# Batch 0 of a gated-attention and mixer kernel: four columns at a time, and the next batch's z turned by TensorE

## The chip, the cores and the metric

The kernel runs on one core of one Trainium2 chip. The metric is the device time of one execution in microseconds (us). The engines are TensorE (PE in the profile, its weight loads PEld), VectorE (DVE), ScalarE (ACT), GpSimd (POOL) and SyncE (SP). POOL issues the plain and the casting DMAs here, SP the DMA transposes.

## The reference: what is computed

There are 8 batches of 3136 rows. All inputs and the output are float32.

```python
# u, v: (8, 3136, 256), z: (8, 3136, 64), U: (3136, 32), V: (32, 3136)
scores = (z @ z.transpose(0, 2, 1)) / 3136
x = u * (maximum(scores, 0) ** 2 @ v)          # gated attention, no softmax
h = x.transpose(0, 2, 1) @ U @ V               # low-rank mixing along the rows
y = x + h.transpose(0, 2, 1)
out = y + maximum(y @ w_ch1, 0) @ w_ch2        # w_ch1: (256, 1024), w_ch2: (1024, 256)
```

## The kernel before: tiles, stages and the order of the work

**Tiles.** A batch's rows make 25 tiles: tile t below 24 holds rows 24p + t for the 128 partitions p (each partition reads 24 rows that lie together), tile 24 the last 64 rows, twice, one copy in each half of the partitions. All matmuls are in bf16. z is kept turned and doubled (`zT`): channels on the partitions, 64 in each half, a tile of 128 columns for each of the 25 tiles, and the first 12 tiles again behind them, so that a window of columns can run past the end (`extend_z`).

**Scores.** The score matrix is symmetric. For tile j, `A[j]` holds 13 blocks of 128 columns: the columns of tiles j, j+1, ..., j+12, round the ring of 25. `score` (line 286) makes a piece of such a row: two matmuls, each on one half of the partitions, into a pair of PSUM banks (`pair_psum`, two pairs in turn), then ScalarE takes relu and scale out of PSUM into `A[j]` (L311), and VectorE squares it in place (L313). `score_steps(b, j, k0, k1)` cuts the blocks k0 to k1 of row j into pieces of up to 1024 columns. The other 12 blocks of a column come by symmetry: `turn` (L333) has SP transpose `A[o]` blocks 1 to 12 into a `strip` (a pool of 5).

**Outputs.** Output tiles are taken in the order 12, 13, ..., 24, 0, ..., 11. "Output i" is the i-th in this order, tile (12 + i) mod 25; so output 8 is tile 20, output 12 is tile 24 and output 13 is tile 0. An output is 25 products with v, each split in two halves of 64 rows (L371), 49 matmuls in all: the first 13 read blocks of `A`, the last 12 the strip. Output 12, the short tile, uses 64x64 pieces (L405). Two outputs share a pair of accumulators; `close_pair` adds the two halves (ScalarE L385, VectorE L386), multiplies by u (L395) and writes x. For the short tile it also adds the two halves of the partitions (L391, L392).

**The list of an output.** Everything is in an order written out by hand. `attend_steps` gives the steps of an output, and `_spread` puts "fill" between them: score pieces that later outputs, or the next batch, need (`own_at`, `next_at`, for batch 0 `first_at`). The strip of output i + 4 is asked for at the end of output i; in batch 0 `first_turns` says which. In batches from 1 on, the mixing and the two weight products of the batch before are done in bursts after outputs 4, 8, 13 and 17 (`burst_at`).

**The start of batch 0** (`start_up`, L665) has no scores to begin with. TensorE is kept busy by 7 dummy matmuls, turns the first 16 tiles of z against a unit matrix (`turn_on_pe`, L223, with a copy out of PSUM by ScalarE or VectorE, L231), and then outputs 0 to 3 are made together: for each pair of tiles j the scores of four columns, then their products (`make`, `use`). The last 9 tiles of z are doubled at step 3 (`double_z`, L188) and turned at step 5. Beside it run the full rows of tiles 16 to 19 (`nxt`). Outputs 4 to 7 follow in the same way (`make_stored`, `use_stored`); here the scores are stored in `A`, and beside them run the rows of tiles 20 to 22 (`more`) and all that rows 8 to 15 still lack (`rest`). After that output 8 begins the regular loop.

**SP's queue** in this stretch is in program order: a small DMA (`mark`, L729) that reads the third part of batch 1's v and so waits until it has landed, strips of tiles 16 to 19, the two transposes of batch 1's z (`turn_z`, L195), strips of tiles 20, 21, and so on.

**POOL's queue** loads in batch 0: v, z, u for two pairs, batch 1's z, the weights (`weight_steps`: w_ch1, U, V, then w_ch2 in two DMAs), three parts of batch 1's v; then u for each pair, with the other six parts of batch 1's v at outputs 9, 11, 13, 15, 18 and 21 (`v_at`). In each later batch the next z is loaded at output 1, doubled in the burst after output 4, and turned at outputs 7 and 10.

The lines of the start-up that the change rewrites (FIRST is 12, NG 4, LEAD 16, NB 13):

```python
        rest = []
        for j in reversed(range(FIRST - NG, LEAD)):
            rest += score_steps(0, j, LEAD + NG - j, NB)
        more = [s for j in range(LEAD + NG, LEAD + 2 * NG - 1) for s in score_steps(0, j)]
...
            if B > 1 and i in (1, 2):
                part = ((0, FIRST), (FIRST, NF))[i - 1]
                double_z(1, (part,))
                turn_z(1, (part,))
            if i == len(pairs) - 1:
                turn(0, LEAD + NG)
```

Of the kernel before, what the change touches and what calls it, by code (L numbers as in the profile page):

```python
# [10 lines left out]
ALU = mybir.AluOpType  # L11
# [31 lines left out]
def kernel(  # L43
# [17 lines left out]
    P = 128  # L61
# [156 lines left out]
    def turn_on_pe(parts, banks):  # L218

        z_bf = z_tiles[0]  # L220
        for (t0, t1), ps in zip(parts, banks):
            for t in range(t0, t1):
# [9 lines left out]
                out=zT_first[:, t0:t1, :].rearrange("p t c -> p (t c)"),  # L232
# [19 lines left out]
    def weight_steps():  # L252
        def wide(w_bf, w):
            pool_dma(out=w_bf, in_=w.rearrange("(t p) d -> p t d", p=P))
# [19 lines left out]
        def copies():  # L274
            for n in (R, 2 * R):
                nc.vector.tensor_copy(out=V_bf[n : 2 * n, :], in_=V_bf[:n, :])

        fetches = [
            lambda: wide(w1_bf, moe_w_ch1),
            narrow,  # L280
            fetch,
            lambda: wide(w2_bf[:, NH // 2 :, :], moe_w_ch2[H // 2 :, :]),
            lambda: wide(w2_bf[:, : NH // 2, :], moe_w_ch2[: H // 2, :]),
        ]
        third = FIRST // 2
        puts = [lambda t=t: put(t, t + third) for t in range(0, NF, third)]
        return fetches, puts + [put_tail, copies]
# [92 lines left out]
    def close_pair(b, o):  # L380
# [8 lines left out]
        if o == NF:  # L389
# [274 lines left out]

    def start_up():  # L665
# [60 lines left out]
        for i, pair in enumerate(pairs):  # L726
# [3 lines left out]
            if i == 3:  # L730
                double_z(0, parts[2:])
            if i == 5:
# [27 lines left out]
        def make_stored(pair):  # L760
            todo = []
            for j in pair:
                k0, k1 = LEAD - j, min(NB, LEAD + NG - j)
                todo.append((j, LEAD * P, (k1 - k0) * P, A[j][:, k0 * P : k1 * P]))
            score(0, todo)

        nxt += [lambda pair=pair: make_stored(pair) for pair in pairs[:2]]
# [8 lines left out]
        rest = []  # L776
        for j in reversed(range(FIRST - NG, LEAD)):
            rest += score_steps(0, j, LEAD + NG - j, NB)
        more = [s for j in range(LEAD + NG, LEAD + 2 * NG - 1) for s in score_steps(0, j)]
        for i, pair in enumerate(pairs):  # L780
            if i + 2 < len(pairs):
                make_stored(pairs[i + 2])
            else:
                more.pop(0)()
            use_stored(pair, outs)
            if B > 1 and i in (1, 2):
                part = ((0, FIRST), (FIRST, NF))[i - 1]
                double_z(1, (part,))
                turn_z(1, (part,))
# [30 lines left out]
    first_at = {8: [(NT - 2, 0, NB), (0, 0, NB)], 9: [(NT - 1, 0, NB)], 10: [(1, 0, NB)]}  # L820
    first_at.update({11: [(2, 0, NB)], 12: []})
    for j, i in zip(range(3, FIRST), (10, 11, 11, 12, 12, 12, 12, 12, 12)):
        first_at[i].append((j, 0, FIRST - j))
    first_turns = {8: (NT - 2,), 9: (NT - 1, 0)}

    next_at = {i: [] for i in range(NT)}
# [119 lines left out]
```

## Time and profile before

| | |
|---|---|
| timed runs (4) | median 1001.18 us, 999.04 to 1002.29 |
| the profiled execution | 998.98 us |
| its span, first to last instruction | 997.2 us |
| mean granted TensorE clock | 0.998 |
| VectorE, ScalarE busy | 550.8, 612.2 us |
| score relu, L311 (ScalarE) | 477 in 358.9 us |
| strips, L333 (SP) | 196 transposes, median 5.4 us from issue to landing |
| DMA | 167.94 MB, mean 168 GB/s |

How to read it: the page gives busy time per engine, a chain of waits followed back from the last instruction, and the costliest groups of instructions by line. A group's line is `line engine op out<-in`, count, busy time and mean, then the engine's idle time before it and what ended it. Windows give busy time of each engine in a stretch, with the count of instructions in brackets, then the granted TensorE clock, the DMA share and GB/s. In the timeline, rows show start, length, engine and line, and in square brackets the idle time before and its releaser. The ring of DMA engines is shared by all queues.

### The profile page before, as it was taken

To read this page: it belongs to the slowest core of one execution; us is meant where nothing else is said; L and a number is where in the kernel's file an instruction comes from. 1 tells how busy PE (TensorE), PEld (TensorE's weight loads), DVE (VectorE), ACT (ScalarE), POOL (GpSimd) and SP (SyncE) were. 2 spreads that over 40 slices of the span, in tenths; PEclk is the share of its full clock that TensorE was granted. 3 is DMA by queue.
4 is the path that set the end of the run, shared out by engine and by line. 5 is a ranking of instruction groups with operands and counts; after the bars stand their busy time and mean duration, and the time that the engine had idled before them with its cause. 6 is when DMAs were issued, how large, how long until landed. Compare 5 with 4: busy or idle time off the path is not lost.

```text
span 997.2 us, 31020 instructions
## 1 busy us (share of the span) xinstructions
PE 984.4 (99%) x13688; PEld 776.4 (78%) x13688; DVE 550.8 (55%) x1003; ACT 612.2 (61%) x835; POOL 171.8 (17%) x317
## 2 busy tenths in 40 slices
PE   8899999999999999999999999999999999999998
PEld 6678777787778878788787887878877788787866
DVE  6868754456544664456644566445664457542352
ACT  7877764667645776456764667556674666643154
POOL 5111112121121111221112211112111120011000
PEclk9999999999999999999999999999999999999999
DMA  9999989999797998899999997989979998678533
GB/s 188 188 188 203 176 151 188 191 176 180 139 210 163 176 155 179 181 184 170 163 179 171 183 170 147 195 173 176 176 150 196 178 176 159 122 153 161 126 96 100
DMA packets 414790, 167.94 MB, mean 168 GB/s; under 512 B 389488, under 2 KB 399408, under 8 KB 414656
## 3 DMA queue, kind: packets, MB, share of 16 engines
q1 hardware_dynamic: 385424, 99.68, 61.8%
q0 software_dynamic: 29232, 66.28, 28.4%
q8 instruction: 107, 1.75, 0.7%
q14 instruction: 27, 0.22, 0.1%
HBM read 61.88 MB, written 25.69 MB: 88 GB/s over the span
## 4 chain that ended last, share of the span: by engine, by line
PE 95%; ACT 2%; DMA 2%; DVE 1%; POOL 0%; issue 0%; DVEq 0%; POOLq 0%
PE ps L371 50%; PE ps L563 17%; PE ps L610 17%; PE ps L298 7%; ACT A L311 2%; PE ps L531 1%; PE ps L405 1%; DMA strip<-A 1%; DMA z_c<-in_z_dram 1%; PE ps L479 1%; DVE A L313 0%; PE ps L462 0%; ACT both L385 0%; POOL v L244 0%; DVE relu_bf L231 0%
## 5 line engine op out<-in xcount | busy, mean ns | idle before, releaser
L311 ACT ACTIVATE A<-ps 128x832 bf16<-128x832 f32 (+9 forms) x477 | 358.9, 769 | 154.6 <-PE ps L298 146.2
L371 PE MATMUL ps<-v,A 64*128 64x256 bf16 x4988 | 341.3, 270 | 1.2 <-DVE A L313 1.1
L313 DVE TENSOR_TENSOR A<-A 128x832 bf16<-128x832 bf16 (+9 forms) x477 | 244.8, 526 | 135.5 <-ACT A L311 133.3
L371 PE MATMUL ps<-v,strip 64*128 64x256 bf16 x4420 | 307.6, 270 | 2.5 <-DMA strip<-A 2.4
L371 PEld LDWEIGHTS <-A 64*128 64x128 bf16 x4988 | 246.1, 94 | 45.8 <-issue 9.5
L581 ACT ACTIVATE relu_bf<-ps 128x1024 bf16<-128x1024 f32 (+2 forms) x206 | 186.2, 911 | 140.2 <-PE ps L563 140.1
L371 PEld LDWEIGHTS <-strip 64*128 64x128 bf16 x4420 | 221.9, 94 | 37.1 <-DMA strip<-A 3.3
L624 DVE TENSOR_TENSOR o_sb<-ps,x_bf 128x512 f32<-128x512 f32 (+2 forms) x105 | 69.8, 665 | 240.3 <-PE ps L610 225.4
L610 PE MATMUL ps<-w_bf,relu_bf 128*128 128x256 bf16 (+1 forms) x1600 | 201.2, 273 | 0.0
L563 PE MATMUL ps<-ut,w_bf 128*128 128x512 bf16 (+2 forms) x896 | 198.6, 353 | 0.0
L610 PEld LDWEIGHTS <-relu_bf 128*128 128x128 bf16 (+1 forms) x1600 | 153.0, 98 | 45.6 <-issue 3.6
L563 PEld LDWEIGHTS <-w_bf 128*128 128x128 bf16 x896 | 84.9, 98 | 62.0 <-issue 6.9
L355 POOL DMA_DIRECT2D u_sb<-in_u_dram x96 | 53.7, 559 | 453.4 <-DVE x_bf L395 438.9
L298 PE MATMUL ps<-zT 64*128 64x416 bf16 (+8 forms) x812 | 131.6, 312 | 0.0
L385 ACT COPY both<-ps 128x512 f32<-128x512 f32 (+1 forms) x104 | 58.9, 566 | 72.2 <-PE ps L371 65.9
L637 POOL DMA_DIRECT2D out_dram<-o_sb x84 | 46.0, 548 | 272.6 <-DVE o_sb L624 269.3
L386 DVE TENSOR_TENSOR both<-ps,both 128x512 f32<-128x512 f32 (+1 forms) x104 | 69.3, 666 | 28.2 <-ACT both L385 27.5
L395 DVE TENSOR_TENSOR x_bf<-both,u_sb 128x512 bf16<-128x512 f32 (+1 forms) x104 | 69.8, 671 | 3.6
L545 DVE TENSOR_TENSOR x_bf<-ps,x_bf 128x512 bf16<-128x512 f32 (+1 forms) x112 | 65.4, 625 | 7.4 <-PE ps L531 7.3
L298 PEld LDWEIGHTS <-zT 64*128 64x128 bf16 x812 | 43.0, 94 | 4.0
L244 POOL DMA_DIRECT2D v<-in_v_dram x61 | 34.1, 561 | 0.8 <-DMA w_bf<-in_moe_w_ch_dram 0.7
L298 PE MATMUL ps<-relu_bf 64*128 64x416 bf16 (+9 forms) x121 | 22.0, 336 | 4.1 <-ACT A L311 3.3
(54 smaller groups left out, 207.1 us busy)
## 6 DMA issues: line engine op xcount, KB each, us to landing
u_sb<-in_u_dram POOLq DMA_DIRECT2D x96, 256.0 KB, 4.0
out_dram<-o_sb POOLq DMA_DIRECT2D x84, 256.0 KB, 3.1
v<-in_v_dram POOLq DMA_DIRECT2D x57, 192.0 KB, 4.7
strip<-A SPq DMA_TRANSPOSE x196, 5.4
out_dram<-o_sb SPq DMA_DIRECT2D x11, 256.0 KB, 2.0
z_c<-in_z_dram POOLq DMA_DIRECT2D x7, 384.0 KB, 5.9
u_sb<-in_u_dram POOLq DMA_DIRECT2D x16, 64.0 KB, 2.3
ut<-x_bf SPq DMA_TRANSPOSE x56, 3.8
```

Source lines behind the costliest of these rows:

```text
L298: mm(out=ps[:, k, :n], lhsT=zT[halves[k], j, :], rhs=zT_flat[halves[k], c : c + n], start=True, stop=True,)
L311: nc.scalar.activation(out=dst, in_=src, func=AF.Relu, scale=sc)
L313: nc.vector.tensor_tensor(out=dst, in0=dst, in1=dst, op=ALU.mult)
L371: mm(out=acc[t0][h][:, (o - t0) * D : (o - t0 + 1) * D], lhsT=w[halves[h]], rhs=v_both[b % 2][halves[h], j, :], start=start, stop=stop, **kw,)
L385: nc.scalar.copy(out=both[:, :w], in_=banks[1][:, :w])
L386: nc.vector.tensor_tensor(out=both[:, :w], in0=banks[0][:, :w], in1=both[:, :w], op=ALU.add)
L395: nc.vector.tensor_tensor(out=x_at(b, t0, n), in0=split(both[:, :w]), in1=u_sb[:, :n, :].rearrange("p t (a c) -> p t a c", c=P), op=ALU.mult,)
L545: nc.vector.tensor_tensor(out=q, in0=split(ps[h][:, : len(ks) * D]), in1=q, op=ALU.add)
L563: mm(out=ps[i][:, :w] if apart else ps[:, i, :w], lhsT=w1_bf[:, db, (hp + i) * P : (hp + i + 1) * P], rhs=uT[c][:, db, len(chunks[c]) * P ...
L581: nc.scalar.activation(out=relus[c][:, hp : hp + 2, :w], in_=ps[:, :, :w], func=AF.Relu)
L610: mm(out=ps[r, k * D : (k + 1) * D], lhsT=relus[c][:, ht, q : q + (TAIL if two else P)], rhs=w2_bf[:, ht, :], start=(ht < 1 + two), stop=( ...
L624: nc.vector.tensor_tensor(out=o_sb[:p].rearrange("p t (a c) -> p t a c", c=P), in0=split(ps[:p, k0 * D : (k + 1) * D]), in1=x_at(b, t, nk) ...
```

## The change

It touches batch 0 and the first outputs of batch 1.

- Batch 1's z is no longer turned by SP in the start-up. It is doubled at output 9 (VectorE) and turned by TensorE, eight tiles at outputs 10, 11 and 13 and one at 14 (`on_pe`), with copies out of PSUM by ScalarE (tiles 0 to 15 and 24) and VectorE (16 to 23). Its 12 repeated tiles are written at output 15 and no longer at 11.
- `make_stored` takes the column from which four outputs' scores are made. `rest` holds only the blocks for outputs 8 to 11, for two rows at a time; the blocks of rows 12 to 15 for later outputs are made at outputs 8 and 9 (`first_more`).
- The rows of tiles 0 to 11 are spread over outputs 10 to 14 (`first_at`), one full row in each of outputs 8 to 12, and the strips are asked for one output later (`first_turns`). Batch 1's rows are made at outputs 16 to 24 (`after_first`) and no longer from 13.
- In the start-up the last 9 tiles of z are doubled at step 4 and turned at step 6, each one step later.
- w_ch2 comes in one DMA, with 8 rows that lie together on each partition, and w_ch1 is loaded into a part of `x_bf` and its columns are put in the matching order by VectorE after outputs 19 and 20 (`order_w`).
- In batch 0 the short tile adds the halves of its partitions straight out of PSUM: four VectorE adds in place of two ScalarE copies and one add.
- The six parts of batch 1's v are loaded at outputs 12, 14, 16, 18 and 20, the short one at 10. Batch 2's z is loaded at output 3 of batch 1 and no longer at output 1.

```diff
--- before.py
+++ after.py
@@ -215,9 +215,9 @@
             nc.vector.tensor_copy(out=z_bf[:, t0:t1, 0, :], in_=z_f)
             nc.scalar.copy(out=z_bf[:, t0:t1, 1, :], in_=z_f)
 
-    def turn_on_pe(parts, banks):
-
-        z_bf = z_tiles[0]
+    def turn_on_pe(parts, banks, b=0):
+
+        z_bf = z_tiles[b]
         for (t0, t1), ps in zip(parts, banks):
             for t in range(t0, t1):
                 mm(
@@ -229,7 +229,7 @@
                 )
             copy = nc.vector.tensor_copy if t0 % 8 or t1 == NF else nc.scalar.copy
             copy(
-                out=zT_first[:, t0:t1, :].rearrange("p t c -> p (t c)"),
+                out=zT_of(b)[:, t0:t1, :].rearrange("p t c -> p (t c)"),
                 in_=ps[:, : (t1 - t0) * P],
             )
 
@@ -250,8 +250,22 @@
     WHOLE = ((0, NF),)
 
     def weight_steps():
-        def wide(w_bf, w):
-            pool_dma(out=w_bf, in_=w.rearrange("(t p) d -> p t d", p=P))
+
+
+        w1_tmp = x_bf[:, NC - 1 :, :].rearrange("p a h -> p (a h)")
+        w1_tmp = w1_tmp[:, : ND * H].rearrange("p (a h) -> p a h", a=ND)
+
+        def first_w():
+            pool_dma(out=w1_tmp, in_=moe_w_ch1.rearrange("(t p) d -> p t d", p=P))
+
+        def second_w():
+            pool_dma(out=w2_bf, in_=moe_w_ch2.rearrange("(p t) d -> p t d", t=NH))
+
+        def order_w(a):
+            nc.vector.tensor_copy(
+                out=w1_bf[:, a, :].rearrange("p (t q) -> p t q", q=P),
+                in_=w1_tmp[:, a, :].rearrange("p (q t) -> p t q", t=NH),
+            )
 
         def narrow():
             pool_dma(out=U_bf[:, :NF, :], in_=rows(moe_U))
@@ -275,16 +289,11 @@
             for n in (R, 2 * R):
                 nc.vector.tensor_copy(out=V_bf[n : 2 * n, :], in_=V_bf[:n, :])
 
-        fetches = [
-            lambda: wide(w1_bf, moe_w_ch1),
-            narrow,
-            fetch,
-            lambda: wide(w2_bf[:, NH // 2 :, :], moe_w_ch2[H // 2 :, :]),
-            lambda: wide(w2_bf[:, : NH // 2, :], moe_w_ch2[: H // 2, :]),
-        ]
+        fetches = [first_w, narrow, fetch, second_w]
         third = FIRST // 2
         puts = [lambda t=t: put(t, t + third) for t in range(0, NF, third)]
-        return fetches, puts + [put_tail, copies]
+        orders = [lambda a=a: order_w(a) for a in range(ND)]
+        return fetches, puts + [put_tail, copies] + orders
 
 
     strips = {}
@@ -386,7 +395,13 @@
         nc.vector.tensor_tensor(
             out=both[:, :w], in0=banks[0][:, :w], in1=both[:, :w], op=ALU.add
         )
-        if o == NF:
+        if o == NF and b == 0:
+
+            for bank in banks:
+                for r in range(2):
+                    q = both[halves[r], :w]
+                    nc.vector.tensor_tensor(out=q, in0=bank[halves[1 - r], :w], in1=q, op=ALU.add)
+        elif o == NF:
             for r in range(2):
                 nc.scalar.copy(out=both[halves[r], w : 2 * w], in_=both[halves[1 - r], :w])
             nc.vector.tensor_tensor(
@@ -661,6 +676,14 @@
         for h in range(1 if j == NF else 2):
             half(0, o, j, h, w, (t0, h) not in begun, stop[h], skip_group_check=True)
             begun.add((t0, h))
+
+    def make_stored(pair, first, n=NG):
+
+        todo = []
+        for j in pair:
+            k0, k1 = first - j, min(NB, first + n - j)
+            todo.append((j, first * P, (k1 - k0) * P, A[j][:, k0 * P : k1 * P]))
+        score(0, todo)
 
     def start_up():
         parts = ((8, 16), (0, 8), (16, NF))
@@ -727,9 +750,9 @@
             if i == 5 and B > 1:
 
                 nc.sync.dma_start(out=mark, in_=v_both[1][:1, V_PARTS[2][1] - 1, :8])
-            if i == 3:
+            if i == 4:
                 double_z(0, parts[2:])
-            if i == 5:
+            if i == 6:
                 turn_on_pe([(16, NF)], [pair_psum().rearrange("p a w -> p (a w)")])
                 turn_on_pe([(NF, NT)], [pair_psum()[:, 0, :]])
                 extend_z(0)
@@ -757,14 +780,7 @@
                     if 0 <= o - j <= HALF:
                         beside(o, j, block(0, o, j))
 
-        def make_stored(pair):
-            todo = []
-            for j in pair:
-                k0, k1 = LEAD - j, min(NB, LEAD + NG - j)
-                todo.append((j, LEAD * P, (k1 - k0) * P, A[j][:, k0 * P : k1 * P]))
-            score(0, todo)
-
-        nxt += [lambda pair=pair: make_stored(pair) for pair in pairs[:2]]
+        nxt += [lambda pair=pair: make_stored(pair, LEAD) for pair in pairs[:2]]
         run(nxt[:2])
         own = [
             lambda j=j, some=some: use_stored([j], some)
@@ -773,20 +789,17 @@
             if j <= some[-1]
         ]
         run(_merge(nxt[2:], own))
-        rest = []
-        for j in reversed(range(FIRST - NG, LEAD)):
-            rest += score_steps(0, j, LEAD + NG - j, NB)
+        rest = [
+            lambda pair=pair: make_stored(pair, LEAD + NG)
+            for pair in zip(range(LEAD - 1, FIRST - NG, -2), range(LEAD - 2, FIRST - NG - 1, -2))
+        ]
         more = [s for j in range(LEAD + NG, LEAD + 2 * NG - 1) for s in score_steps(0, j)]
         for i, pair in enumerate(pairs):
             if i + 2 < len(pairs):
-                make_stored(pairs[i + 2])
+                make_stored(pairs[i + 2], LEAD)
             else:
                 more.pop(0)()
             use_stored(pair, outs)
-            if B > 1 and i in (1, 2):
-                part = ((0, FIRST), (FIRST, NF))[i - 1]
-                double_z(1, (part,))
-                turn_z(1, (part,))
             if i == len(pairs) - 1:
                 turn(0, LEAD + NG)
         tail = []
@@ -817,17 +830,24 @@
     for j, i in enumerate((6, 7, 8, 9, 3, 5, 4, 2, 9, 8, 7, 6)):
         own_at[i].append((j, 0, FIRST - j))
 
-    first_at = {8: [(NT - 2, 0, NB), (0, 0, NB)], 9: [(NT - 1, 0, NB)], 10: [(1, 0, NB)]}
-    first_at.update({11: [(2, 0, NB)], 12: []})
-    for j, i in zip(range(3, FIRST), (10, 11, 11, 12, 12, 12, 12, 12, 12)):
+    first_at = {8 + n: [(t, 0, NB)] for n, t in enumerate((23, 24, 0, 1, 2))}
+    first_at.update({13: [], 14: []})
+    for j, i in zip(range(3, FIRST), (10, 11, 12, 13, 13, 13, 14, 14, 14)):
         first_at[i].append((j, 0, FIRST - j))
-    first_turns = {8: (NT - 2,), 9: (NT - 1, 0)}
-
+    first_more = {8: (LEAD - 1, LEAD - 2), 9: (LEAD - 3, LEAD - 4)}
+    first_turns = {8: (23,), 9: (24,), 10: (0,), 11: (1,), 12: (2,), 13: (3, 4)}
+
+    on_pe = {10: (0, 8), 11: (8, 16), 13: (16, NF), 14: (NF, NT)}
     next_at = {i: [] for i in range(NT)}
     for j in range(FIRST):
         next_at[max(NB, FIRST + j)].append((j, FIRST - j, NB))
     for j, i in enumerate((14, 15, 16, 18, 19, 20, 24)):
         next_at[i].append((FIRST + j, 0, NB))
+    after_first = {i: [] for i in range(NT)}
+    for j, i in enumerate((16, 16, 17, 17, 18, 18, 19, 20, 21, 22, 23, 24)):
+        after_first[i].append((j, FIRST - j, NB))
+    for j, i in enumerate(range(16, 23)):
+        after_first[i].append((FIRST + j, 0, NB))
 
     def run(steps):
         for s in steps:
@@ -835,7 +855,7 @@
 
     fetches, puts = weight_steps()
     start_up()
-    puts = dict(zip((13, 14, 15, 16, 17, 18), puts))
+    puts = dict(zip((13, 14, 15, 16, 17, 18, 19, 20), puts))
     late = []
     for b in range(B):
         more = b + 1 < B
@@ -843,22 +863,33 @@
         bursts = bursts_of(b - 1) if b else []
         burst_at = {4: (0, 1), 8: (2, 3), 13: (4, 5), 17: (6, 7)}
         own = own_at if b else first_at
-        v_at = dict(zip((9, 11, 13, 15, 18, 21), V_PARTS[3:]))
+        v_at = dict(zip((12, 14, 16, 18, 20, 10), V_PARTS[3:]))
         ahead = dict(zip((2, 3, 6, 7, 10, 11, 14), range(NC)))
         for i in range(begin, NT):
             o = turns(i)
             fill = [s for key in own.get(i, ()) for s in score_steps(b, *key)]
+            if b == 0 and i in first_more:
+                fill.append(lambda pair=first_more[i]: make_stored(pair, LEAD + 2 * NG))
             if more:
-                fill += [s for key in next_at[i] for s in score_steps(b + 1, *key)]
-                if b and i == 1:
+                coming = next_at if b else after_first
+                fill += [s for key in coming[i] for s in score_steps(b + 1, *key)]
+                if b and i == (1 if b > 1 else 3):
                     load_z(b + 1, WHOLE)
+                if b == 0 and i == 9:
+                    double_z(b + 1, ((FIRST, NF), (0, FIRST)))
                 if b and i == 7:
                     turn_z(b + 1, ((FIRST, NF),))
                 if b and i == 10:
                     turn_z(b + 1, ((0, FIRST),))
+                if b == 0 and i in on_pe:
+                    fill.append(
+                        lambda part=on_pe[i]: turn_on_pe(
+                            [part], [pair_psum().rearrange("p a w -> p (a w)")], 1
+                        )
+                    )
                 if b == 0 and i in v_at:
                     load_v(b + 1, v_at[i])
-                if i == 11:
+                if i == (11 if b else 15):
                     extend_z(b + 1)
             main = attend_steps(b, o)
             if b and i in ahead:
```

## The prediction

> **What bounds the kernel now.** I read the page first. TensorE (PE) is busy for nearly the whole span, so a gain has to be less TensorE work or a TensorE wait that goes.
>
> ```profile
> span 997.2 us, 31020 instructions
> PE 984.4 (99%) x13688; PEld 776.4 (78%) x13688; DVE 550.8 (55%) x1003; ACT 612.2 (61%) x835; POOL 171.8 (17%) x317
> ```
>
> The profiled execution took 998.98 us, 1.78 more than this span. The four timed runs have a median of 1001.18 us (999.04 to 1002.29), 2.2 above it; I sum against the profiled execution and then move the difference to the median. Runs of one kernel here lie up to 0.2% from their median, so a change under 0.2% can't be told from none.
>
> The chain of waits is 95% TensorE, and stretches of 20 us show it at 20.00 of 20.00 us from 80 us to the last 100 us. Nothing can be won there. From 0 to 80 us it is at 16 to 19 of 20. The list of TensorE's waits to 70 us says for whom:
>
> ```profile
> PE ps L298 <- ACT A L311: 3.3, 5, 1.0
> PE ps L371 <- DMA strip<-A: 2.4, 1, 2.4
> PE ps L371 <- DVE A L313: 1.1, 3, 0.5
> ```
>
> The dearest single wait is for a strip. The windows of 2 us around it (TensorE busy is the second number, the granted clock the last but two):
>
> ```profile
> 46.00:48.00 2.00, 0.88 (x16) 0.56 (x10) 1.97 (x4) 1.46 (x2) 0.46 (x1) 1.00 1.30 321
> 48.00:50.00 2.00, 0.72 (x12) 0.60 (x14) 0.25 (x1) 0.00 (x1) 0.63 (x2) 1.00 1.22 260
> 50.00:52.00 2.00, 2.00 (x22) 1.39 (x18) 0.59 (x1) 1.41 (x2) 0.00 (x0) 0.50 0.81 148
> 52.00:54.00 2.00, 2.00 (x27) 1.48 (x23) 0.59 (x1) 0.55 (x2) 0.00 (x0) 0.65 1.20 162
> 54.00:56.00 2.00, 2.00 (x40) 1.77 (x36) 0.59 (x1) 1.38 (x2) 0.00 (x0) 1.00 1.28 273
> ```
>
> The reader is to see two losses: 46 to 50 us with TensorE idle for 2.4 us, and then 3.3 us (50.0 to 53.3) at half the clock. The timeline of 35 to 50 us shows what made the strip late.
>
> ```profile
> 39.60 3.33 SPq L195 DMA_TRANSPOSE zT<-z_bf  x2
> ...
> 43.02 7.02 SPq L333 DMA_TRANSPOSE strip<-A  x3
> ...
> 49.28 0.50 PE L371 MATMUL ps<-v,strip 64*128 64x256 bf16 x6 [2.39 <-DMA strip<-A]
> ```
>
> SP's queue ran four strips (tiles 16 to 19), then batch 1's two z transposes (L195), and only then, at 43.02, tile 20's strip, whose row had been ready at about 37.3 (its last square on VectorE). It landed at 49.23.
>
> To put a number on every stretch I set the instructions in program order beside their starts and gave each a bare cost from undisturbed rows: a product L371 53.3 ns (output 13: 49 products and 384 score columns in 2.71 us), score columns 1/4.8 ns each (two matmuls of 416 columns at 49.62, next start 49.79), a turned z tile 55 to 57 ns (below). Actual against bare, us: start-up (1.26 to 44.91) 43.65 against 30.91; output 8 6.73 against 3.31; output 9 3.95 against 2.96; output 10 3.22 against 3.20; output 11 3.58 against 3.36; output 12 4.23 against 1.87; outputs 13 to 24 36.68 against 35.86. So 20.6 us of batch 0 are not bare work: 12.7 in the start-up, 4.4 in outputs 8 and 9 (the strip and the clock), 2.4 in output 12.
>
> **Part 1, z of batch 1 by TensorE.** Removed: the two z transposes of SP. Without them tile 20's strip is issued when tile 19's issue ends (39.5; some 38.6 with the start-up changes) and, as the transpose that stood there landed 4.3 us after its issue (39.60 to 43.88), it lands at about 43 to 44. It is wanted 1.7 us into output 8, at about 44.6. The wait goes, and the slow clock with it: **-4.4**, leaving 0.3 in the two outputs. What is late next is tile 21's strip, wanted 3.2 us later and queued 2.5 behind: no wait. The Trainium skill bears on the clock (TensorE: Matmul & The Clock Gate, "The HAM clock gate"): half rate comes after an idle window of about 3.4 us, free-running. The row shows it after a 2.4 us gap, so the row decides; if the page's length were needed, the slow clock would have another cause and 1.8 of the 4.4 would stay.
>
> Added: 25 matmuls of 128x128. The price is in batch 0's own late z tiles:
>
> ```profile
> 11.56 0.51 PEld L223 LDWEIGHTS <-z_bf 128*128 128x128 bf16 x9 [0.54 <-DVE z_bf L188]
> ...
> 11.56 0.68 PE L223 MATMUL ps<-eye,z_bf 128*128 128x128 bf16 x9 [0.26 <-DVE z_bf L188]
> ...
> 12.28 0.27 ACT L231 CAST relu_bf<-ps 128x128 bf16<-128x128 f32 x1 [0.91 <-PE ps L223]
> ...
> 12.59 0.39 PE L298 MATMUL ps<-relu_bf 64*128 64x512 bf16 x2 [0.35 <-ACT relu_bf L231]
> ...
> 12.69 1.22 DVE L231 CAST relu_bf<-ps 128x1024 bf16<-128x1024 f32 x1
> ```
>
> Nine weight loads take 0.51, so 57 ns a tile: 25 cost **+1.4**, none hidden, since TensorE is the bound there. The copies: tiles 0 to 7 and 8 to 15 by ScalarE (1024 columns, not in the trace on ScalarE for a copy; L311 of 1024 columns is spaced 0.92, taken; 0.8 to 1.1 would hardly matter), tiles 16 to 23 by VectorE (1.22 above), tile 24 by ScalarE (0.27). They hold a score bank. In outputs 10 and 11 ScalarE then has 3.5 and 3.8 us of work (row 1.52, partial row 1.1 and 0.92, copy 0.92, pair copy 0.47) against TensorE's bare 3.63 and 3.60: level, I take 0.6 of waits (0 to 1.5, a whole bank wait in each). In output 13 VectorE carries the tail's close (four adds of 64x256, each near the 0.43 of L490, in place of one, 0.43), three squares, the 1.22 copy and a put of 0.82, so the bank comes back about 0.8 late to output 14: **+0.8** (0 to 1.5). Doubling z at output 9 is four VectorE copies, 1.5 us; squares queue behind it, but nothing reads them for two outputs.
>
> **Part 2, the start-up.** Batch 0's late z: in the rows above TensorE stood behind the doubling and then the copies, 0.48, 0.52 and 0.32 us between starts, and ScalarE idled 2.2 us from 11.4 to 15.5. Doubling one step later and turning one later puts score work between. From 15.5 to 34 ScalarE is full, so at most 2.2 is won; but the strips of tiles 16 to 19 wait for the mark (29.82, batch 1's third v part), and TensorE already waits for the first at 36.33. The mark moves by the DMA time only: w2 was 1024 packets of 512 B at 60 ns, 3.8 us of 16 queues' time; now 128 of 4096 B, by the packets of 1536 to 3072 B (136 to 273 ns) about 360 ns, 2.9 us. So **-0.9** (0 to -2.2). Panel 2's tail: "rest" shrinks from 36 blocks to 26. ScalarE's spacing for the eight old pieces is 4.4 us, for the eight new ones 3.3, and ScalarE is full from 38 to 46 us: **-1.0** (0 to -1.1), 0.3 of it bare.
>
> **Part 3, output 12.** Six partial rows there are cut to one and row 2 is added: twelve score matmuls become six. Each change between the 64x64 products and scores costs some 0.17 us, and one wait for ScalarE is 0.54:
>
> ```profile
> 64.51 0.28 PE L298 MATMUL ps<-relu_bf 64*128 64x256 bf16 x2 [0.54 <-ACT A L311]
> ```
>
> I take 1.4 over bare in place of 2.36: **-1.0** (0 to -1.6). The ten blocks of tiles 12 to 15 and the row shifts move bare work to outputs 8, 9, 13 and 14 without adding any.
>
> **Part 4, batch 1's rows in outputs 16 to 24, and the rest.** Score columns are the same in sum, but outputs 17 to 22 now hold 2560 to 3072 columns each. By its spacings ScalarE needs 2.6 to 3.0 us there, TensorE 3.15 to 3.25 bare: **+0.3** (0 to 1.0). The two w1 reorders on VectorE (1024 strided columns; L265 takes 0.82 for 768) are about 1.1 each at outputs 19 and 20, out of chunks of x_bf first written at output 23; VectorE was busy 1.2 to 2.0 of 2, and only squares wanted in batch 1 queue behind, so 0. The tail's pair of ScalarE copies (0.82) goes, inside output 13, 0. v loads on POOL stand behind u loads that wait for VectorE; all land by output 22, first use is batch 1: 0. Batch 2's z moves behind one u load in batch 1: issue about 113.8 for 106.6, landing about 121, before its doubling at 124.6: 0; if it were 5 us later VectorE would hold up a pair's close.
>
> Sum: -4.4 + 1.4 + 0.3 (outputs 8, 9 and small) + 0.6 + 0.8 - 0.9 - 1.0 - 1.0 + 0.3 = -3.9; all best ends together give -7.6, all worst +1.3. I round to **-4**: 995 for the profiled execution, **997.2** for the median.
>
> **Rivals.**
> - *The start-up and outputs 8 to 12 run at ScalarE's pace.* If strips 16 to 19 come as early as ScalarE lets TensorE arrive, the 2.2 us, the whole tail and output 12 are won and no wait is added: the best ends, -7.6, 993.6. For it: ScalarE is full in both. Against: the mark. Chance 0.15.
> - *The waits come back at ScalarE and VectorE.* Outputs 10 to 14 and 17 to 22 stall at their upper ends, 1.5 + 1.5 + 1.0 in place of 1.7: -1.6, 999.6. For it: ScalarE and TensorE level in outputs 10 and 11. Against: outputs 13 to 24 lose only 0.8 in all today. Chance 0.15.
> - *Slower: the strips of tiles 0 to 3 come late.* They are released one output later than now. Tile 2's row is scored half way through output 12 (about 59), ready near 61.7, and with the 7.1 us of today (63.69 to 70.78) lands at 68.8, wanted in the middle of output 15, about 69. If landings grow to 10 us, tiles 1 and 2 each cost a gap of 2.6 and 1.8 of slow clock: +8.8 - 4 = +4.8, 1006. It decides from about 9.5 us of landing. Against: SP has two transposes fewer. Chance 0.10.
> - *The change doesn't do what it says* in one point: tile 20's strip is late still, because its row or the DMA engines and not SP's order held it: -4 + 4 = 0, 1001. Against: its row was ready 5.7 us before the issue. Chance 0.03.
>
> **Numbers.** Forecast 0.57 (-2.5 to -6: 995.2 to 998.7), the rest as above. Leaving out the slower case and some of the first rival, the range goes from 992.8 to the case without effect, 1001.2. Faster by over 0.2% (under 999.2): 0.57 + 0.15 = 0.72; within: 0.15 + 0.03 = 0.18; slower: 0.10.
>
> **What would show it.** Tile 20's strip issued before 40 us and no DMA strip wait over 0.5 us after output 8; clock 1.00 from 6 us on; output 8 under 3.8 us; output 12 near 3.2; batch 1's first product near 99.3 instead of 103.3. A strip wait in outputs 13 to 15, a clock under 1.00, or over 1 us of waits for ScalarE in outputs 17 to 22 would make it wrong.

## The result and the profile after

The changed kernel took 1003.32 us (median of 54 runs, 997.57 to 1013.52) beside 1000.85 us for the kernel before (76 runs): a ratio of **1.0022, 95% interval 1.0011 to 1.0033**. It is slower by a fifth of a per cent; 997.2 us was forecast, in a range of 992.8 to 1001.2. Its profiled execution took 999.36 us.

The head of its page, then its list of waits from 6 to 75 us (waiter, releaser: us in total, times, longest):

```profile
span 997.6 us, 31073 instructions
PE 983.7 (99%) x13709; PEld 779.4 (78%) x13709; DVE 554.1 (56%) x1013; ACT 614.1 (62%) x840; POOL 170.2 (17%) x316
```

```profile
PE ps L307 <- ACT A L320: 2.2, 3, 1.0
...
PE ps L307 <- DVE zT L231: 1.3, 1, 1.3
...
PE ps L380 <- DVE A L322: 1.1, 3, 0.5
...
PE ps L380 <- DMA strip<-A: 1.1, 1, 1.1
```

The wait of 2.4 us for tile 20's strip is gone (the 1.1 left is tile 16's, at 36.59). In its place is one wait of 1.3 for the copy of the turned z, at 67.46. In the windows where before stood still (TensorE busy is the second number, the granted clock the last but two) nothing stands now, and the clock is full:

```profile
46.00:48.00 2.00, 2.00 (x38) 1.88 (x36) 2.00 (x5) 1.70 (x4) 1.12 (x3) 1.00 1.07 272
48.00:50.00 2.00, 2.00 (x41) 1.95 (x39) 2.00 (x6) 1.70 (x3) 0.47 (x1) 1.00 0.96 191
50.00:52.00 2.00, 2.00 (x39) 1.98 (x35) 1.97 (x6) 2.00 (x5) 0.00 (x0) 1.00 1.07 179
```

SP's queue shows why: the six strips follow each other with nothing between them.

```profile
32.86 13.04 SPq L342 DMA_TRANSPOSE strip<-A  x6
```

So in batch 0 the strip wait and the slow clock went as forecast, and batch 1's first product starts at 100.69 instead of 103.30 (99.3 was forecast). The table sets the starts of the batches' first products side by side, and shows where the 2.61 us went:

| | batch 1 | 2 | 3 | 4 | 5 | 6 | 7 | span |
|---|---|---|---|---|---|---|---|---|
| before | 103.30 | 224.29 | 345.27 | 466.26 | 587.25 | 708.40 | 829.39 | 997.2 |
| changed | 100.69 | 223.09 | 344.16 | 465.15 | 586.83 | 708.59 | 829.57 | 997.6 |

An undisturbed batch is 120.99 long in both. The changed kernel loses 1.41 in batch 1, 0.69 in batch 4 and 0.77 in batch 5, where none of TensorE's instructions differs: 2.9 us in all (before: 0.2), more than the 2.6 that were won. A repeat (e1, profiled at 1005.14 us) shows the same in large, in its timeline from 145 to 168 us:

```profile
149.57 0.55 POOL L652 DMA_DIRECT2D out_dram<-o_sb  x1 [2.39 <-DVE o_sb L639]
...
156.80 0.49 PE L380 MATMUL ps<-v,strip 64*128 64x256 bf16 x6
...
161.34 0.69 DVE L639 TENSOR_TENSOR o_sb<-ps,x_bf 128x512 f32<-128x512 f32 x1 [9.23 <-DMA out_dram<-o_sb]
...
162.08 2.96 PE L380 MATMUL ps<-v,A 64*128 64x256 bf16 x26 [4.80 <-DVE o_sb L639]
```

The store issued at 149.57 lands at 161.22. There are two buffers for o_sb (the tile that the stores send out), so VectorE waits 9.23 us to write the next; the squares that stand behind it in VectorE's queue come late, and TensorE waits 4.80. Then the clock is at half for 6.83 us.

### The profile page after: what moved, and what is told of

It reads as the page before. It is cut to its first block, busy times and chain, and to the rows that moved or that the text cites. A ratio compares the mean times of both kernels' runs of the same rounds, so it can differ in the third digit from the quotient of the medians.

```text
span 997.6 us, 31073 instructions
## 1 busy us (share of the span) xinstructions
PE 983.7 (99%) x13709; PEld 779.4 (78%) x13709; DVE 554.1 (56%) x1013; ACT 614.1 (62%) x840; POOL 170.2 (17%) x316
## 3 DMA queue, kind: packets, MB, share of 16 engines
q8 instruction: 107, 1.75, 0.8%
## 4 chain that ended last, share of the span: by engine, by line
PE 92%; DMA 3%; ACT 2%; DVE 2%; issue 1%; POOL 0%; DVEq 0%; POOLq 0%
PE ps L380 49%; PE ps L625 17%; PE ps L578 17%; PE ps L307 7%; ACT A L320 1%; PE ps L546 1%; PE ps L420 1%; DMA zT<-z_bf 1%; DMA out_dram<-o_sb 1%; DMA v<-in_v_dram 1%; PE ps L494 1%; DMA strip<-A 1%; DMA ut<-x_bf 0%; DVE A L322 0%; DVE x_bf L560 0%
## 5 line engine op out<-in xcount | busy, mean ns | idle before, releaser
L380 PEld LDWEIGHTS <-A 64*128 64x128 bf16 x4988 | 247.9, 94 | 45.3 <-issue 10.7
L307 PE MATMUL ps<-zT 64*128 64x416 bf16 (+9 forms) x812 | 132.0, 312 | 0.0
```

Source lines behind the costliest of these rows:

```text
L307: mm(out=ps[:, k, :n], lhsT=zT[halves[k], j, :], rhs=zT_flat[halves[k], c : c + n], start=True, stop=True,)
L380: mm(out=acc[t0][h][:, (o - t0) * D : (o - t0 + 1) * D], lhsT=w[halves[h]], rhs=v_both[b % 2][halves[h], j, :], start=start, stop=stop, **kw,)
```

## The experiments

"Row offset" below is how many rows more than before stand on TensorE's queue ahead of batch 1 (a matmul is two: load and multiply). The change itself adds 42. "Loss" is a batch's length over 120.99 us in the profiled execution, which is one execution of each kernel; ratios come from 12 runs of each (6 in e9, e10, e12, e13 and e16; 54 of the changed kernel) against those of before on the same chip.

| kernel | offset | ratio (95%) | batch 1 starts | loss in batch 1 | loss in 2 to 6 |
|---|---|---|---|---|---|
| before, as first shown | 0 | 1 | 103.30 | 0.0 | 0.2 |
| e8 before again, one run | 0 | (1009.33 us) | 104.08 | 2.7 | 6.5 |
| e17 before itself | 0 | 0.9997 (0.9970-1.0024) | 102.34 | 0.0 | 1.8 |
| e18 before | 256 | 0.9985 (0.9959-1.0011) | 103.90 | 0.0 | 0.0 |
| e5 before | 42 | 1.0031 (1.0004-1.0058) | 102.27 | 0.0 | 5.8 |
| e11 the same | 42 | 1.0051 (1.0023-1.0079) | 106.21 | 0.5 | 6.3 |
| e12 before | 128 | 1.0066 (1.0040-1.0092) | 106.57 | 0.0 | 2.4 |
| e16 before | 192 | 1.0074 (1.0056-1.0093) | 105.69 | 0.0 | 5.1 |
| changed | 42 | 1.0022 (1.0011-1.0033) | 100.69 | 1.4 | 1.5 |
| e1 changed again | 42 | 1.0024 (1.0002-1.0045) | 100.13 | 7.8 | 1.5 |
| e2 batch 2's z at 1 | 42 | 1.0034 (1.0011-1.0058) | 100.17 | 2.9 | 7.5 |
| e3 v as before | 42 | 1.0026 (1.0005-1.0047) | 100.53 | 0.2 | 4.7 |
| e4 weights as before | 42 | 1.0030 (1.0005-1.0054) | 100.38 | 1.4 | 2.0 |
| e6 changed | 256 | 0.9998 (0.9970-1.0027) | 99.48 | 7.0 | 10.2 |
| e13 the same | 256 | 1.0059 (1.0036-1.0081) | 101.97 | 8.6 | 3.0 |
| e7 z by SP | -8 | 1.0020 (0.9996-1.0044) | 99.33 | 3.9 | 7.4 |
| e14 changed | 128 | 1.0036 (1.0012-1.0060) | 101.49 | 2.4 | 2.7 |
| e15 changed | 192 | 1.0026 (1.0010-1.0043) | 100.94 | 1.8 | 7.8 |

**One part put back at a time (e1 to e4).** My first theory, A, was that the new order of batch 1's rows leaves its strips too little time at the change of batches: in the changed kernel's profile some strips of outputs 20 to 26 landed 0.3 to 2.3 us ahead of use, 5 to 9 in before. Against it, B: the stores and transposes of the later batches come late. e1 changes nothing; the edits of e2, e3 and e4 are:

```
-                if b and i == (1 if b > 1 else 3):          # e2
+                if b and i == 1:
-        v_at = dict(zip((12, 14, 16, 18, 20, 10), V_PARTS[3:]))   # e3
+        v_at = dict(zip((9, 11, 13, 15, 18, 21), V_PARTS[3:]))
-        fetches = [first_w, narrow, fetch, second_w]        # e4, with wide() as in before, no orders
+        fetches = [lambda: wide(w1_bf, moe_w_ch1), narrow, fetch, ...]
```

> The changed kernel once more, unchanged, for a second trace and a second set of times. Theory A (thin strips): the profiled execution of the changed kernel is 2.6 us ahead of before when batch 1 begins, but its strips for outputs 21 to 26 of the count from batch 0's start land only 0.3 to 2.3 us ahead of their use, where before had 5 to 9; in most executions some land late, and a wait of over 2 us also halves the clock. Then this set has a median of 1.002 of before, a good part of its executions with a mean clock of 0.998 or less, and these some 4 us longer than the others. Theory B (later batches): the loss is spread over batches 1 to 6 in waits under 1 us that keep the clock; then clock and time do not go together, and this trace again shows only small waits after batch 1 begins.

> Undoes one part: batch 2's z is loaded at output 1 of batch 1, as before. Theory C: the load at output 3 stands among the first transposes and stores of batch 1 and makes the turned x at 122 us and the store at 158 us late, 0.5 and 0.8 us in the profile of the changed kernel; then this is 1 to 1.5 us faster than the changed kernel in the same job, ratio to before near 1.001, and the two waits are gone. Theory A: no difference from the changed kernel beyond 0.5 us.

> Undoes one part: batch 1's v is loaded at outputs 9, 11, 13, 15, 18 and 21, as before. Theory A with its cause in the v loads (they stand right behind the u loads from 65 to 86 us, when the strips need the DMA engines): strips for outputs 21 to 26 get 3 us or more of margin, executions with a clock under 0.999 become rare, and the median falls by 3 to 5 us, to 0.997 to 0.999 of before. If the v loads are not the cause: margins stay under 2.5 us and the ratio stays near 1.002.

> Undoes one part: both weights come as before (w_ch2 in two DMAs of 512 B pieces, no reordering of w_ch1 by VectorE after outputs 19 and 20). Theory A with its cause in VectorE (it is busy 4.9 of 5 us from 85 to 95 us with the two reorders, and POOL's DMA issues take 0.8 to 1.0 us there in place of 0.55): strip margins at outputs 22 to 26 grow by 2 us or more and the median falls by 2 us or more. If not: the same margins, the mark lands up to 0.9 us later, and the ratio stays at 1.002 or 1 us above.

Measured: 1.0024, 1.0034, 1.0026 and 1.0030. None of the three edits brings anything back. In all four traces, the strips of outputs 20 to 26 whose landing is recorded land 2.5 to 8.7 us ahead of use, and no strip keeps TensorE after batch 1 has begun; yet batches 1 to 6 lose 3.4 to 10.3. A falls, and so does the theory C of e2, since the ratio stayed (what e2 did mend is told below). The waits over 0.45 us of these later batches are for VectorE's o_sb or x_bf, and one for ut, x turned by a transpose of SP for the weight products.

**What is common to them: rows (e5 to e8).** The page lists a queue that the prediction passed over:

```profile
q8 instruction: 107, 1.75, 0.8%
```

That is one packet of 16384 B for each 256 rows of TensorE's queue (27,376 in before). What one does to the transfers, shown in the 10 us of e1 around the late store (40 slices of 0.25 us; the fetch is at 155.4):

```profile
DMA  6998999589999931000999994418879999999199
GB/s 49 128 132 77 115 138 116 67 241 434 200 156 188 91 5 16 0 17 17 70 205 102 350 92 56 75 25 82 218 273 384 194 227 184 175 263 158 32 265 293
...
q8 instruction: 1, 0.02, 1.0%
```

From 1 us behind the fetch hardly anything moves for 1.3 us. Over the 739 such fetches from 100 to 940 us of the eight traces of before and its variants with rows, the bytes of all other queues fall from some 190 KB a us to 71 to 90 between 0.5 and 1.75 us behind the fetch's start and are back at 178 from 2.0: each costs the transfers about as much as 0.9 us without any. So theory D: the 42 rows move each fetch 42 rows forward against batches 1 to 7, and with it onto other stores and transposes. e5 gives before 42 rows by cutting its 7 warm-up matmuls into 28 with the same columns in all, e6 fills the changed kernel's offset up to one whole fetch, e7 takes the turned z out again (eight rows fewer than before), e8 is a second trace of before:

```
-        for _ in range(7):
-            mm(out=ps[:, 0, :], lhsT=zT_rest[:, 0, :], rhs=wide, start=True, stop=True)
+        for _ in range(28):                                  # e5, in before
+            mm(out=ps[:, 0, :P], lhsT=zT_rest[:, 0, :], rhs=wide[:, :P], ...)
+        for _ in range(114):                                 # e6, in the changed kernel
+            mm(out=ps[:32, 0, :32], lhsT=zT_rest[:, 0, :32], rhs=wide[:, :32], ...)
```

```
-                if b == 0 and i in on_pe:                    # e7
-                    fill.append(lambda part=on_pe[i]: turn_on_pe(...))
+                if b == 0 and i in (10, 11):
+                    turn_z(1, (((FIRST, NF), (0, FIRST))[i - 10],))
```

> The kernel before, with the seven warm-up matmuls of 512 columns at the start cut into 28 of 128 columns (same columns, 42 more rows on TensorE's queue, as many as the changed kernel has more); nothing else differs. Theory D (the phase of TensorE's instruction fetches, one packet of 16384 B per 256 rows, decides which stores and transposes of the later batches come late): batches 1 to 6, 726.1 us from batch 1's first product to batch 7's in the trace of before, take 3 to 9 us more, as in the changed kernel; batch 0 stays as it is; ratio 1.003 to 1.007. Rival S (SP has two transposes fewer and other timing in batch 0, and the rows do not matter): ratio 1.000, batches 1 to 6 as in a second trace of before. Rival R (the losses of later batches come by chance in both kernels): 1.000, with losses in this trace that a second trace of before has too.

> The changed kernel, with the seven warm-up matmuls of 512 columns cut into 114 of 32 columns with 32 columns of weights (214 more rows; with the change's 42 that is 256, so each fetch stands again at the instruction of before). Theory D: batches 1 to 6 lose no more than in before, ratio 0.997 if the start-up isn't lengthened, up to 1.000 if the many small matmuls take up to 3 us longer there. Rivals S and R: the same losses as in the changed kernel, 1.002 to 1.005.

> The changed kernel without its part 1: batch 1's z is turned by two transposes on SP's queue at outputs 10 and 11 (as late as that, so they can't hold the strip of tile 20), not by 25 matmuls on TensorE. TensorE has 8 rows fewer than before, so its fetches stand almost as before. Theory D: batches 1 to 6 as in before, batch 0 3 to 5 us shorter (the 1.4 us of the matmuls, the 1.3 us wait at output 14 and some 0.6 at outputs 10 and 11 go, if no strip comes late for the two transposes): ratio 0.995 to 0.997. Rival S: also 0.995 to 0.998, since SP has its two transposes again. Rival R: batch 0 shorter and the later losses at random, 0.997 to 1.000. If strips of outputs 13 to 15 come late behind the transposes, batch 0 gives some of it back.

> The kernel before, unchanged, for a second trace. Theory D and rival S: batches 1 to 6 take 726 us, within 1 us, and the wait for tile 20's strip (2.4 us) and the half clock after it are there again. Rival R: batches 1 to 6 take 2 to 8 us more than in the first trace, with the same waits of VectorE for stores as in the changed kernel.

Measured: e5 1.0031, by rows alone; its list of waits from 100 to 940 us holds a wait for a store that the first trace of before doesn't have:

```profile
PE ps L371 <- DVE o_sb L624: 2.9, 1, 2.9
PE ps L405 <- DVE x_bf L545: 0.7, 2, 0.4
```

e6 came to 0.9998, for D, though its profiled execution (1012.4) lost 17 us. e7 is against D in its simple form: at an offset of -8 it should have been near 0.996 and was 1.0020. e8 shows that before loses too in some executions (9.2 us in this one): the first trace, 0.2 us of loss, was a lucky one, and the losses come in some executions and not in others.

**The v loads moved out of the bursts (e9, e10).** If stores come late because v loads stand before them on POOL's queue, loads put elsewhere should help both kernels.

```
-                    loads = [lambda k=k: load_v(b + 1, V_PARTS[k]) for k in ...]
-                    steps = _merge(steps, loads)
+                for k in apart_at.get(i, ()) if b else ():   # at outputs 5, 6, 9, 10, 14, 15, 18, 19
+                    load_v(b + 1, V_PARTS[k])
```

> The changed kernel, with the v loads of batches 2 to 7 taken out of the bursts of the second stage, where they stand on POOL's queue between the stores, and put behind outputs 5, 6, 9, 10, 14, 15, 18 and 19 instead; all else as in the changed kernel. Theory C (in batches 1 to 6 the stores, the v loads and SP's transposes meet in the bursts, stores land up to 11 us after their issue, VectorE waits for one of the two o_sb buffers and TensorE behind it; batch 0's gain of 2.6 to 3.2 us is real and is lost there): no wait of TensorE for o_sb over 0.5 us, batches 1 to 6 take 726 to 728 us, ratio 0.995 to 0.998. Rival (the stores come late for SP's transposes alone, or the losses have another site): batches 1 to 6 still 728 to 735 us, ratio 1.000 to 1.003.

> The kernel before with the same move of the v loads. Theory C: before loses a median of 1 to 2 us in batches 1 to 6 in this way, so ratio 0.998 to 0.999, and it stays 2 to 3 us above the changed kernel with the move; the wait for tile 20's strip and output 12 are as before. Rival: 1.000.

Measured: **1.0200** (1.0175 to 1.0225) and **1.0173** (1.0142 to 1.0204). Theory C falls, and by far: batches 1 to 6 lose 30 and 22 us. In e9 TensorE waits in each of the six for VectorE's x_bf, 1.0 to 5.9 us at a time, 15.9 in sum. Why the loads do more harm there I did not follow.

**Offsets (e11 to e16).** The same cut of the warm-up matmuls, with other counts: e11 is e5 again; e12 71 of 48 columns and e16 103 of 35, in before; e13 is e6 again; e14 50 of 72 and e15 82 of 44, in the changed kernel.

> The same kernel as e5_before_42_rows, once more, because the first interval hardly left 1.000. Theory D (the phase of TensorE's instruction fetches sets how often the later batches lose): again 1.002 to 1.006, at least half of the runs with a half clock episode. Rival R (by chance): 0.999 to 1.001.

> The kernel before with the seven warm-up matmuls cut into 71 of 48 columns with 48 columns of weights: 128 more rows, half a fetch. Theory D: another rate of loss than before's, in either direction, ratio off 1.000 by 0.2% or more. Rival R: 1.000, but for up to 1 us more in the start-up.

> The kernel of e6_after_214_rows once more (row offset against before 256, the same phase as before). Theory D: 0.996 to 1.000, under the changed kernel's 1.0022. Rival R: 1.002.

> The changed kernel with the seven warm-up matmuls cut into 50 of 72 columns with 72 columns of weights: with the change's own 42 rows an offset of 128 rows, as in e12_before_128_rows (1.0066). Theory D (the offset of the rows sets the losses of batches 1 to 6; the change itself is worth 2.6 to 3.2 us at any offset): some 0.3% under e12, 1.002 to 1.005, and not under the changed kernel itself. Rival (the change itself makes the later losses): 1.002 as the changed kernel or above e12.

> The changed kernel with 82 warm-up matmuls of 44 columns: an offset of 192 rows. Theory D: a value of its own between 0.995 and 1.006, some 0.3% under e16. Rival: 1.002 as the changed kernel.

> The kernel before with 103 warm-up matmuls of 35 columns: an offset of 192 rows, as e15. Theory D: off 1.000 again (0.998 to 1.007), some 0.3% above e15. Rival: 1.000.

Measured: before is slower at 42, 128 and 192, by 0.3 to 0.7%. The changed kernel stands under it at each equal offset: 1.0022 to 1.0024 against 1.0031 and 1.0051 (42), 1.0036 against 1.0066 (128), 1.0026 against 1.0074 (192, the only one whose intervals are apart). That is D's 0.3%, within a wide error. But e13 contradicts e6: the same kernel, 1.0059 after 0.9998. At the offset of before the changed kernel does not go to 0.997. Nor is all of it in the later batches, where D put it: in e11, e12 and e16 batch 1 starts 2.4 to 3.3 us later than in the first trace of before, and 0.8 to 2.2 us of that is in output 16 of batch 0. In e12 ScalarE waits there for the transpose of a strip, and TensorE 2.0 us for ScalarE:

```profile
80.34 2.22 ACT L311 ACTIVATE A<-ps 128x640 bf16<-128x640 f32 x3 [3.38 <-DMA strip<-A]
```

**Is it the offset, or any added row, or the way it is measured (e17, e18)?** e17 is before unchanged, e18 has 135 warm-up matmuls of 26 columns, exactly one fetch more.

> The kernel before, unchanged, timed as a variant against the kernel before. Theory D, and any theory of the kernel: 1.000 (0.998 to 1.002). Rival M (a program run as the variant is slower by 0.3 to 0.6% whatever it is, so that the other ratios here are that much too high): 1.003 to 1.006.

> The kernel before with 135 warm-up matmuls of 26 columns: 256 more rows, so each fetch of TensorE's instructions stands at the instruction where it stood in before. Theory D: 1.000, at most 1.001 for the start-up, well under the 1.0066 and 1.0074 of 128 and 192 rows. Rival N (any added row costs, by the start-up or by another mechanism, and the offset modulo 256 is nothing): 1.006 to 1.009.

Measured: 0.9997 and **0.9985** (0.9959 to 1.0011). With 42, 128 and 192 rows before loses, with 256 it doesn't. So neither added rows as such nor the many small matmuls (e18 has the most) cost time; what is left is the offset within a fetch. The 256 rests on one set of 12 runs, and e6 and e13 show how far two sets of one kernel can lie apart. In e18 the list of TensorE's waits from 100 to 940 us has no entry.

## Why the prediction was wrong

**What held.** The strip wait and the slow clock: outputs 8 and 9 had 4.4 us over bare (the prediction's cost of the work without waits) and have 0.2 (forecast 0.3 left). Output 12: 2.36 over bare became 1.00 (forecast 1.4). The start-up in sum: 43.65 became 42.31, in e1 41.58 (forecast -1.9, measured -1.3 and -2.1), though not by its term for the mark, the small DMA that holds SP's strips: -0.9 was forecast, and it was issued at 30.36 in the changed kernel and 29.14 in e1, beside 29.82, 30.56 and 30.12 in three traces of before (first, e8, e17). The term is smaller than that spread. Outputs 10 and 11: 0.96 over bare (forecast 0.6 more than 0.24). Outputs 17 to 22: no loss where 0.3 was put.

Mis-sized: the copy of z tiles 16 to 23 on VectorE, +0.8 forecast; TensorE waits 1.29 for it and output 14 is 1.80 over bare, where it was 0.12. Batch 1 starts at 100.1 to 100.7, not 99.3. One thing in it was not as solid as the one profile made it: of 35 runs of before beside e1 to e4, 13 had a mean clock of 1.000, so the slow clock's part of the 4.4 (half of 3.41 us, 1.7) wasn't there to win in every run.

**The step that failed** is the first one: "stretches of 20 us show it at 20.00 of 20.00 us from 80 us to the last 100 us. Nothing can be won there." (Behind 300 us the stretches were of 100 us, full as well.) I read it as: nothing can be lost there either. The sum had no term for batches 1 to 7, because their instructions do not change, and moved the 2.2 us between profile and median along as a constant. But e8 and e17 show that before too loses 9.2 and 1.8 us in its later batches in some executions, which its first profiled execution happened not to do; the changed kernel and its variants lose 2.9 to 17.2 us there in their ten traces. Two things that the change moves bear on this:

- *The row offset* (shown for before, not for the changed kernel). 42 rows alone make before 0.3 to 0.5% slower, 256 rows nothing. Before stands at an offset that suits it; of the four others tried with rows alone, only the one that is the same modulo 256 is as good. That is 3 to 5 us, as much as the change wins; the prediction counted the 25 matmuls at 57 ns each, 1.4 us, and nothing for their rows. But it isn't shown that the changed kernel lost its gain in this way: in batches 2 to 6 its five traces at offset 42 (the first, e1 to e4) lose 3.5 in the mean, three of before unchanged 2.8 (0.2, 6.5, 1.8), and with the offset set back the ratios are 0.9998, 1.0059 and 1.0020 (e6, e13, e7), not the 0.997 of theory D.
- *Batch 1* (in part shown). In ten traces of the changed kernel and its variants batch 1 loses 0.2 to 8.6 us, 3.7 in the mean; in eight of before and its variants 0.4 in the mean, whatever the offset. Two waits make most of it. In six of the ten TensorE waits 0.65 to 4.8 us for a store 58 to 64 us into batch 1 (16.4 us in all; in e1, e6 and e13 the half clock follows); none of the eight has this wait in batch 1. Why the store is late there is not shown. And in five of the ten TensorE waits for ut at the first burst (0.7 to 2.6 us at a time, 9.7 in all), in none of the eight. Here are TensorE's wait, the time from issue to landing and SP's rows there in e13, where z comes late, and the last two in e2, where it is put back:

```profile
  DMA ut<-x_bf: 2.9, 2
...
DMA to landing us min/median/max: 5.9/6.4/6.9
...
113.82 1.23 SPq L519 DMA_TRANSPOSE ut<-x_bf  x1
115.15 3.86 SPq L342 DMA_TRANSPOSE strip<-A  x1
119.06 1.31 SPq L519 DMA_TRANSPOSE ut<-x_bf  x1
```

```profile
DMA to landing us min/median/max: 3.2/4.2/5.2
...
112.02 1.23 SPq L519 DMA_TRANSPOSE ut<-x_bf  x1
113.34 1.49 SPq L342 DMA_TRANSPOSE strip<-A  x1
114.89 1.65 SPq L519 DMA_TRANSPOSE ut<-x_bf  x1
```

Batch 2's z, issued 3.3 us into batch 1 in before and e18, is issued 10.4 us into it in e13, and its three transfers land at 16.5 to 17.0: beside the first ut, which is issued at 11.9 and lands at 17.7 where it was 15.1. The strip behind it is held up too, so the second ut is issued at 17.1 and not at 14.7. It lands at 24.0, with loads of u and v issued just behind it (17.3 and 17.8), and the wait of 2.64 is for this one. In all nine traces with the late z the second ut is issued at 16.3 to 17.5; in e2 and the eight of before and its variants at 14.7 to 15.4. So moving z is what makes ut late. I had put that move at 0, because z itself is not late; I didn't ask what it would run beside. It is not the whole of the batch's loss: e2 still lost 2.9, at the store, and at its offset of 42 none of the four traces with the late z waits over 0.4 us for ut in batch 1. z put back at another offset wasn't tried.

So the balance by the profiles at hand: -2.6 and -3.2 in batch 0 (the changed kernel's two traces), +3.3 in batch 1 (the means, 3.7 against 0.4), and in batches 2 to 6 nothing that these traces can tell from the spread of before. That makes +0.1 to +0.7; the medians differ by 2.5, and these traces do not account for the rest. What stays open: why the changed kernel at the offset of before (e6, e13, e7) loses 3 to 10 us in batches 2 to 6, when before there loses 0 to 2 in three of four traces. VectorE and ScalarE have 10 and 5 instructions more by the pages, so the fetches of other engines (8192 B, 28 in the changed kernel's span) moved as well: in batch 1 one stands at 52.7 us in the changed kernel and at 45.3 in before. Whether that makes the store of batch 1 late, or the losses behind it, wasn't tried. The spread of one kernel (e6 and e13, 0.6% apart with intervals that don't meet) is also wider than the intervals say. No version here beat before by more than its interval.

Of the rivals, none was this. "The waits come back" came true in output 14 alone, which lost 1.7 us more than before; outputs 10, 11 and 17 to 22 stayed off their upper ends, and 999.6 was its time. "Slower" had the direction, by a path that didn't happen: no strip of outputs 13 to 16 is late, the changed kernel's land 1.1 to 5.1 us ahead of use.

## What to carry to other kernels

When one profile shows a stretch without any loss, compare its time with the median of the runs: if runs are longer, look for losses in that stretch that come and go; a change elsewhere can move their rate though no instruction there changes. Before crediting or blaming a change of a few tenths of a per cent, shift the kernel by some rows on the queue of the engine with most instructions and time it: here that alone was worth -0.1 to +0.7% for the kernel before, more than the change. And of a transfer that is moved, ask not only when it is wanted but which transfers run in its new place.

## What the runs showed of the hardware

- **Instruction fetches share the DMA engines.** TensorE's come once in 256 rows, one packet of 16384 B in about 1.0 us (the median of 18 traces). In the 10 us of e1 above the one packet took 1.0% of the 16 engines' time, but behind a fetch the bytes of all other queues fall from some 190 KB a us to 71 to 90 for over a us. The 60 fetches of 8192 B that stood alone in the same eight traces cost 0.3 to 0.5 us of traffic, by the stretch that one compares with.
- **The half clock comes in units, and not by the length of the gap alone.** From output 8 of batch 0 to the start of batch 7 it lasted 3.41 or 6.83 us each time in the twenty traces. Of fifteen gaps of 2.1 to 3.2 us on TensorE it came after eight (2.12, 2.25, 2.39 and 3.06 among them) and not after seven (2.24, 2.70 and 3.11 among them); after each of the ten gaps from 3.4 us up it came. The Trainium skill (TensorE: Matmul & The Clock Gate, "The HAM clock gate") gives an idle window of about 3.4 us that runs freely; the unit of 3.41 agrees with it, the drops after 2.1 to 2.4 us of idling don't.
- **Packets of transfers slow down in bunches.** From 148 to 160 us of e1, around the late store, strip packets of 256 B took 51 ns in the mean, though 71% of them took 20 or less (the median of the whole trace is 18); POOL's packets of 4096 B took 450 in the mean and 191 in the median, beside 166 in the median of the whole trace. What slows them is not shown.
